# Holding back woven-in steps ahead of a long attention visit, loading two gate factors a unit earlier, and dealing the first score fills 4, 3, 3

## The chip, the cores and the metric

The kernel runs on one core of a Trainium2 chip. Its time is the device time of one execution in microseconds (us), median of several runs. The core has five engines that work side by side, each through its own instructions in order: TensorE (PE in the profile; PEld is its weight load), VectorE (DVE), ScalarE (ACT), GpSimd (POOL) and SyncE (SP, which here only issues DMAs). TensorE writes its results into PSUM, which this kernel uses as eight banks of 128 partitions x 512 floats; a bank can be written again once the engines that read it are done.

## The reference

All in float32, with x of 2048 x 640:

```
q, k, v = x wq, x wk, x wv           # 32 heads of 20, in 4 segments of 512 rows
per segment s and head:
    a_dot = softmax(q k^T / sqrt(20) + causal mask) v
    a_mem = (phi(q) M) / (phi(q) z + 1e-6)        # phi(t) = t+1 if t>0 else exp(t)
    o     = g a_mem + (1 - g) a_dot               # g = sigmoid(beta), per head
    M    += phi(k)^T v ;  z += sum phi(k)
a   = o wo
b   = (silu(x w1) * (x w3)) w2                    # inner width 1728
out = G a + (1 - G) b                             # G = sigmoid(x . gate_w), per row
```

## The kernel before, in words

The 2048 rows are four chunks of 512 (a chunk is a segment); the chunks go in two pairs, A = (0, 1) and B = (2, 3). A value that needs more precision than one pass gives is held as a high and a low part, and a product is three passes over them (`PASSES`), so a 640-wide projection of one 128-column block is 5 x 3 = 15 matmuls of 128 x 512.

Two streams of work share TensorE. The first is dense work: projections q, k, v; the feed-forward part (`ffn_up`, tiles g and u; `ffn_down`, tile f); the output projection (`oproj`, tile op); and small pieces woven into them. The second is attention, four heads (a *unit*) after another, 32 units. The order on TensorE is the order in which the Python code emits it; the order on the other engines is chosen by the framework's scheduler when the kernel is built.

**Attention visits.** `attention` (L792 on) counts slots, 40 to a unit. In slot 5 stands the *long visit* (`BIG`): three s fills, four t fills and the o product. In slot 17 stands the *short visit* (`SMALL`): s, t, s. An s fill (L634) puts scores of two heads into two banks, and VectorE scans them for row maxima (L641). A t fill (L667) puts transposed scores into two banks; ScalarE takes their exponential into P (L673) and GpSimd masks it (L677). The o product (L687) takes one bank. Unit 1 is an exception: its slot 5 has the first three fills only, and a further visit in slot 11 has the other four.

**Banks.** `bank_tile` gives the eight banks in turn: the one given longest ago comes next. A dense accumulation *holds* its bank until its last matmul, when `filled` puts it at the end of the row.

**Slots and credit.** The main loop at the end of the function gives, after every slot, a credit (declared cost of the segment's dense work divided by its slots) and draws dense steps while the credit is positive. A step is mostly three matmuls and declares 699 ns. Ahead of a visit of four or more pieces (place "between") it draws up to eight steps more, until no bank is held; ahead of a smaller one ("amid") up to four, until a bank has been held for two steps. What is drawn there is taken off the credit that follows.

**Weaving.** `braid(a, b, every, skip, rest)` yields the steps of a and puts one step of b behind every so many of them. Woven in like this are:

- `normalize` (L761 to L769; tiles rr, gt, on): for each of five 128-row blocks one matmul of row factors (rr), for chunks 1 to 3 also four transposes of memory's part (gt), each in a bank of its own; VectorE multiplies and adds (L762, L767), ScalarE casts (L768), VectorE subtracts (L769). In unit 10 for chunk 0, unit 19 for chunk 1, units 26 and 27 for chunk 2, and in the tail for chunk 3.
- `memory_read` (tile nd, L352): eight steps of six matmuls with three small VectorE operations each. In units 0 and 1 for chunk 1, 16 and 17 for chunk 2, 19 to 21 for chunk 3.
- `split_x` (L130 to L132, tile xh): x of chunks 2 and 3 is split into high and low parts, in unit 12 and at the start of 13.
- `load_memory` (L749): memory's part is loaded through GpSimd's queue.

**Gate factors.** `load_share(c)` (L740) loads the factors of chunk c, spread over 128 partitions (tile sh), on ScalarE's DMA queue. `share` (L543) multiplies the result by them. For chunk 0 it is called when its last `ffn_down` starts, for chunk 1 when the output projection starts after normalization, for chunks 2 and 3 in the tail.

## Time and profile before

| | |
|---|---|
| median of 3 runs | 1105.04 us (1104.69 to 1105.52) |
| profiled execution | 1107.25 us |
| its span on the core | 1105.4 us |
| TensorE clock granted in it | 1.00 |
| busy: PE / DVE / POOL / ACT | 1094.9 / 598.1 / 584.6 / 381.3 us |
| DMA | 153.20 MB, 139 GB/s mean |

The profile is one execution. A row of its timeline has the start in us from the start of the span, the duration, the engine, the line of the kernel, the operation, the tile written and those read, the shape and the number of merged instructions; in brackets stands how long the engine had been idle and what ended that. Matmuls are pipelined: each of 128 x 512 shows some 0.4 us, but the next starts after 0.23. So where time is lost on TensorE is read from start to start, not from its busy time.

### The profile page before, as it was taken

The page shows a single profiled execution, that of the slowest core. Times are in us where ns is not written, and L with a number is a line of the kernel's source. Part 1 is how long each engine was busy: PE and PEld are TensorE (multiplying, and loading weights), DVE is VectorE, ACT ScalarE, POOL GpSimd, SP SyncE. Part 2 cuts the span into 40 slices and gives each one's busy share as a digit, 9 for nine tenths or more (in the row PEclk, how much of TensorE's full clock was granted, in tenths as well). Part 3 has the DMA queues.
Part 4 walks back from the last instruction along what each step waited for, and adds up shares of the span by engine and source line. Part 5 has one row for each costly group of instructions (what it writes and reads, how often), then busy time and mean ns, then how long its engine had stood idle before and what let it go on. Part 6 is the DMA issues. An engine that isn't in the chain of part 4 may idle for free.

```text
span 1105.4 us, 17904 instructions
## 1 busy us (share of the span) xinstructions
PE 1094.9 (99%) x6290; PEld 853.0 (77%) x6290; DVE 598.1 (54%) x1711; ACT 381.3 (34%) x826; POOL 584.6 (53%) x729
## 2 busy tenths in 40 slices
PE   9999999999999999999999999999999999999998
PEld 6988877777777777787977777777777777777787
DVE  5032564356555554366153678875557665651575
ACT  6244233343233122145244543325333332223020
POOL 5055556366366363565066447556774665655263
PEclk9999999999999999999999999999999999999999
DMA  8256943334355134435367966365664343433122
GB/s 306 110 205 220 281 125 82 95 82 116 77 142 129 51 84 123 126 94 171 121 197 265 288 215 183 97 161 146 151 159 109 85 116 96 117 103 89 52 79 95
DMA packets 87545, 153.20 MB, mean 139 GB/s; under 512 B 11584, under 2 KB 25184, under 8 KB 87456
## 3 DMA queue, kind: packets, MB, share of 16 engines
q1 hardware_dynamic: 63040, 106.30, 30.1%
q0 software_dynamic: 20384, 38.68, 15.9%
q10 hardware_dynamic: 4032, 7.08, 1.8%
q8 instruction: 50, 0.82, 0.3%
q14 instruction: 39, 0.32, 0.1%
HBM read 96.56 MB, written 54.54 MB: 137 GB/s over the span
## 4 chain that ended last, share of the span: by engine, by line
PE 93%; DVE 4%; ACT 1%; DMA 1%; issue 1%; ACTq 0%; SPq 0%; DVEq 0%
PE g L257 16%; PE f L580 16%; PE u L257 16%; PE k L257 6%; PE v L385 6%; PE op L837 6%; PE o L687 6%; PE q L257 5%; PE s L634 5%; PE t L667 4%; PE nd L352 1%; PE pm L449 1%; PE q L327 1%; DVE junk L641 1%; DMA sh<-ed 1%
## 5 line engine op out<-in xcount | busy, mean ns | idle before, releaser
L641 DVE CUSTOM_DVE_ANT_0 junk<-s,mask 128x256 bf16<-128x256 f32 (+3 forms) x512 | 250.3, 489 | 105.9 <-PE s L634 73.6
L673 ACT ACTIVATE P<-t 128x512 f32<-128x512 f32 (+1 forms) x384 | 172.5, 536 | 190.2 <-PE t L667 153.0
L257 PE MATMUL g<-X,W 128*128 128x512 f32 x840 | 208.5, 398 | 0.0
L179 POOL TENSOR_TENSOR W<-wr,W 128x640 fp32r<-128x640 f32 (+1 forms) x126 | 198.5, 1581 | 2.5
L174 POOL CAST W<-wr 128x640 fp32r<-128x640 f32 (+1 forms) x126 | 92.5, 739 | 202.0 <-PE f L580 47.7
L580 PE MATMUL f<-ht,W 128*128 128x512 f32 (+1 forms) x825 | 197.0, 395 | 0.7 <-DVE acc L550 0.7
L257 PE MATMUL u<-X,W 128*128 128x512 f32 x780 | 196.7, 399 | 0.0
L677 POOL TENSOR_SCALAR_AFFINE_SELECT P<-P 128x256 f32<-128x256 f32 x192 | 94.6, 502 | 183.2 <-ACT P L673 182.9
L257 PEld LDWEIGHTS g<-X,W 128*128 128x128 f32 x840 | 155.9, 188 | 36.6 <-issue 0.4
L580 PEld LDWEIGHTS f<-ht,W 128*128 128x128 f32 x825 | 152.9, 188 | 37.6 <-DVE acc L550 1.5
L257 PEld LDWEIGHTS u<-X,W 128*128 128x128 f32 x780 | 144.0, 188 | 34.4 <-ACT P L673 0.3
L107 POOL TENSOR_TENSOR ht<-ft,ht 128x512 fp32r<-128x512 f32 x52 | 67.2, 1291 | 90.1 <-ACT ht L106 90.0
L611 POOL DMA_DIRECT2D qk<-qkd x128 | 83.6, 655 | 0.5 <-issue 0.2
L634 PE MATMUL s<-qk 60*128 60x256 f32 (+3 forms) x512 | 77.8, 345 | 1.1 <-DVE fu L520 1.0
L257 PE MATMUL k<-X,W 128*128 128x512 f32 x300 | 77.0, 403 | 0.0
L687 PE MATMUL o<-P,vg 128*32 128x512 f32 (+3 forms) x1024 | 75.5, 435 | 1.4 <-DVE on L767 1.4
L519 ACT ACTIVATE ft<-g 128x512 f32<-128x512 f32 x52 | 31.2, 599 | 124.9 <-PE g L257 113.8
L385 PE MATMUL v<-W,X 128*128 128x320 f32 (+1 forms) x480 | 71.9, 311 | 0.3 <-ACT P L673 0.3
L520 DVE SCALAR_TENSOR_TENSOR fu<-ft,g 128x512 f32<-128x512 f32 x52 | 35.7, 686 | 67.3 <-ACT ft L519 58.3
L385 PEld LDWEIGHTS v<-W,X 128*128 128x128 f32 x480 | 71.0, 189 | 1.0 <-ACT P L673 0.5
L106 ACT CAST ht<-ft 128x512 fp32r<-128x512 f32 x52 | 32.2, 619 | 110.9 <-DVE ft L528 110.8
L588 DVE TENSOR_TENSOR acc<-f,acc 128x512 f32<-128x512 f32 x65 | 44.7, 689 | 44.8 <-PE f L580 44.6
(123 smaller groups left out, 1204.8 us busy)
## 6 DMA issues: line engine op xcount, KB each, us to landing
qk<-qkd POOLq DMA_DIRECT2D x128, 240.0 KB, 4.0
wr<-in_w_dram SPq DMA_DIRECT2D x80, 320.0 KB
qkd<-qs SPq DMA_DIRECT2D x20, 512.0 KB
qkd<-ks SPq DMA_DIRECT2D x20, 512.0 KB
od<-oq SPq DMA_DIRECT2D x32, 256.0 KB
wr<-in_wo_dram SPq DMA_DIRECT2D x20, 320.0 KB
vg<-vd SPq DMA_DIRECT2D x16, 336.0 KB
xr<-in_xT_dram SPq DMA_DIRECT2D x20, 256.0 KB
```

The source lines that it names most:

```text
L107: (lo or nc.gpsimd.tensor_sub)(dst[:, 1], src, dst[:, 0].bitcast(F32))
L174: hi = nc.gpsimd.tensor_copy(w[:, 0, :n], raw[:, :n])
L179: last["low"] = nc.gpsimd.tensor_sub(w[:, 1, :n], raw[:, :n], w[:, 0, :n].bitcast(F32))
L257: nc.tensor.matmul(ps, w[:, a, kb * P:(kb + 1) * P], x[:, b, kb, :], start=n == 0, stop=n == 14)
L385: nc.tensor.matmul(ps[:, :n1 - n0], x[:, a, kb, lb * P:(lb + 1) * P], wvt[kb][:, b, n0:n1], start=n == 0, stop=n == 14)
L580: nc.tensor.matmul(ps[:, :n1 - n0], w, h, start=n == 0, stop=n == len(ms) - 1)
L611: here(nc.gpsimd.dma_start(t[64 * i:64 * i + RH], qkd[c][RH * (h + i):RH * (h + i + 1)]))
L634: nc.tensor.matmul(ps[i][:, o:o + w], q[:, qb * P:(qb + 1) * P], key[:, :w], start=n == 0, stop=n == len(todo) - 1, skip_group_check=True)
L641: nc.vector.tensor_tensor_reduce(out=junk[:, :w], in0=ps[i][:, o:o + w], in1=mask[:, L - w:], scale=1.0, scalar=-3.0e38, op0=ALU.add, op1= ...
L673: last["exp"] = nc.scalar.activation(pairs[2 * m + k]["P"][:, i, o:o + n], ps[i][:, b:b + n], AF.Exp, scale=SCALE)
L677: nc.gpsimd.affine_select(d, d, pattern=[[0, 2], [0, n], [1, P]], base=0, channel_multiplier=-1, compare_op=ALU.is_ge, fill=0.0)
L687: nc.tensor.matmul(ps[32 * i:32 * i + 32, kb * P:], heads[2 * p + i]["v"][:, kb], pairs[p + i // 2]["P"][:, i % 2, o:o + n], start=kb == 0 ...
```

## The change

Three edits. First, `braid` counts the woven-in steps that are due, and emits one only while `near()` is false; `near()` is true while the slot counter stands at 2 to 5 of a unit, that is in the draws after slots 1 to 4 and in those made ahead of the long visit in slot 5. A step that fell due there comes behind a later step of a, one at a time. Second, the factors of chunk 0 are loaded ahead of the last up projections of pair A, those of chunk 1 ahead of chunk 1's normalization; for chunks 2 and 3 the call stays where it is, in a function that takes the chunks. Third, in unit 1 the fill ("t", 1, 3) moves from the visit in slot 11 to that in slot 5, so that unit 1's three visits have four, three and three fills; by their sizes the first now counts as "between" and the second as "amid".

```diff
@@ ffn_down
         for c in cs:
-            if c in last and c < 2:
-                load_share(c)
             if first:
@@
-    def both_shares():
-        for c in B:
+    def load_shares(cs):
+        for c in cs:
             load_share(c)
             yield 1
@@ attention
-                todo = VISITS.get(n, ()) if m != 1 else {BIG: VISITS[BIG][:3], BIG + 6: VISITS[BIG][4:]}.get(n, VISITS.get(n, ()))
+                todo = VISITS.get(n, ()) if m != 1 else {BIG: VISITS[BIG][:3] + VISITS[BIG][4:5], BIG + 6: VISITS[BIG][5:]}.get(n, VISITS.get(n, ()))
@@ oproj
         def first():
+            if c == 1:
+                load_share(c)
             yield from normalize(c)
...
         def rest():
             ws.extend(w_get(i, plan[0]) for i in plan)
-            if c == 1:
-                load_share(c)
@@
+    def near():
+        return BIG - 3 <= (slots - LEAD) % 40 <= BIG
+
     def braid(a, b, every, skip=0, rest=True):
 
         def gen():
-            n = 0
+            n = due = 0
             for y in a[1]:
                 yield y
                 n += not isinstance(y, float)
-                if n > skip and (n - skip) % every == 0:
+                due += n > skip and (n - skip) % every == 0
+                if due and not near():
+                    due -= 1
                     z = next(b[1], None)
                     if z is not None:
                         yield z
@@
     A, B = (0, 1), (2, 3)
+    slots = 0
@@ segment of pair A's end
-    seg += [(0, load_raw(2)), (0, load_raw(3))] + u0 + [braid(chain(u1), (0, x2), 4, 0, False)]
+    seg += [(0, load_raw(2)), (0, load_raw(3)), (0, load_shares(A[:1]))] + u0 + [braid(chain(u1), (0, x2), 4, 0, False)]
@@ tail
-    tail = [braid(chain([d, (0, both_shares())] + u), o1, 4, 10)] + [braid(o2, (0, shared(2)), 3), job_down(B, 4, B)]
+    tail = [braid(chain([d, (0, load_shares(B))] + u), o1, 4, 10)] + [braid(o2, (0, shared(2)), 3), job_down(B, 4, B)]
@@ main loop
-    slots, credit = 0, 0.0
+    credit = 0.0
```

## The prediction

> **What bounds the kernel now.** I read the page's engine shares and chain first, then the list of TensorE's waits, then the timeline of TensorE around each named place, and last VectorE's timeline there.

> ```profile
> span 1105.4 us, 17904 instructions
> PE 1094.9 (99%) x6290; PEld 853.0 (77%) x6290; DVE 598.1 (54%) x1711; ACT 381.3 (34%) x826; POOL 584.6 (53%) x729
> PE 93%; DVE 4%; ACT 1%; DMA 1%; issue 1%; ACTq 0%; SPq 0%; DVEq 0%
> ```

> TensorE is busy for the whole span and carries 93% of the chain of waits. The change keeps all 6290 matmuls, so only the time between their starts can move. The undisturbed pace is the yardstick: rows of unit 18 (long visit, short visit) and two rows of projection work.

> ```profile
> 679.59 0.50 PE L634 MATMUL s<-qk 60*128 60x512 f32 x2
> 684.09 3.73 PE L257 MATMUL g<-X,W 128*128 128x512 f32 x15
> 689.14 0.50 PE L634 MATMUL s<-qk 60*128 60x256 f32 x4
> 690.10 1.20 PE L257 MATMUL u<-X,W 128*128 128x512 f32 x4
> ...
> 473.39 7.13 PE L257 MATMUL g<-X,W 128*128 128x512 f32 x30
> 480.36 1.54 PE L257 MATMUL u<-X,W 128*128 128x512 f32 x6
> ```

> From start to start, a long visit takes 684.09 - 679.59 = 4.50 us, a short one 690.10 - 689.14 = 0.96 us, and thirty wide matmuls 6.97 us, 0.232 us each. What lies above this is waiting, and little of it is left in the whole trace; the change aims at three places.

> **Part 1, the first t fills (unit 1).** The second visit of unit 1 has four fills now:

> ```profile
> 152.60 0.50 PE L667 MATMUL t<-qk 62*128 62x512 f32 x2
> 153.41 0.33 PE L634 MATMUL s<-qk 60*128 60x384 f32 x1
> ...
> 153.99 0.68 DVE L520 SCALAR_TENSOR_TENSOR fu<-ft,g 128x512 f32<-128x512 f32 x1
> 154.72 0.50 PE L634 MATMUL s<-qk 60*128 60x384 f32 x3 [0.98 <-DVE fu L520]
> ```

> Four fills take eight banks. The eighth is the bank that the g projection has just closed, and VectorE's fu (0.68) still reads it. The two matmuls of this pair normally start together; here they are 154.72 - 153.41 = 1.31 us apart. Some 1.25 us is lost. With three fills in this visit only six banks are taken and that wait goes: -1.25. In its place the first visit takes all eight banks and comes right after u: its last t fill needs u's bank, and the memory step that the pause puts behind it needs the bank of the first s fill, which VectorE must scan first. No row shows this order. Lower bound 0 (VectorE's work fits), upper bound 1.31 (the same wait, moved). I take 0.5: one VectorE operation like that fu, 0.68, is ahead of that scan, and I guess 0.2 of it covered. Part 1: -0.75, between -1.25 and +0.06.

> **Part 2, the gate factors.** Chunk 0's load (sh) is issued when the down projection starts, and VectorE, first in first out, stops at its first use:

> ```profile
> 495.39 9.38 PE L580 MATMUL f<-ht,W 128*128 128x512 f32 x40
> 496.37 0.32 ACTq L740 DMA_DIRECT2D sh<-ed  x1
> 503.12 1.29 DVE L543 TENSOR_TENSOR acc<-acc,sh 128x512 f32<-128x512 f32 x2 [3.35 <-DMA sh<-ed]
> 505.07 1.44 PE L580 MATMUL f<-ht,W 128*128 128x512 f32 x5 [0.30 <-DVE acc L550]
> 512.34 0.51 PE L634 MATMUL s<-qk 60*128 60x512 f32 x2
> 517.85 1.45 PE L385 MATMUL v<-W,X 128*128 128x320 f32 x8 [0.30 <-ACT P L673]
> ...
> 495.39:517.85 22.46, 18.09 (x34) 1.00 0.48 161
> ```

> The load takes 503.12 - 496.37 = 6.75 us; VectorE idles 3.35 of them. TensorE pays later, when it needs banks: from 495.39 to 512.34 stand 65 wide matmuls, 15.1 us at 0.232, in 16.95 us: 1.85 lost. The long visit of unit 13 takes 5.51 instead of 4.50: 1.01 lost. Together 2.86. Issued ahead of the two g projections, at about 473.39, the load has 23 us more, over three times its 6.75, even beside the raw inputs loaded just before; ScalarE's issue is 0.32 us as before. The last row (a stretch; VectorE busy for 18.09 of 22.46 us) shows that VectorE can keep up once the hole is closed: 4.37 us are idle, 3.35 of them the hole. What stays: it runs with little slack, two splits of x now fall behind the visit, and the v projection then starts on a bank that waits for a scan instead of an exponential. I leave 0.86 for that, between 0 and 2.0 (the 1.01 of the visit and half of the 1.85). Part 2: -2.0, between -2.86 and -0.86. Chunk 1's factor causes no wait now, and the last two loads stay where they are: 0.

> **Part 3, the pause.** Normalization in unit 19:

> ```profile
> 699.88 0.39 PE L761 MATMUL rr<-rR,sel 96*128 96x512 bf16 x1
> 701.33 0.50 PE L634 MATMUL s<-qk 60*128 60x512 f32 x2
> 702.85 0.68 DVE L767 TENSOR_TENSOR on<-on,gt 128x512 f32<-128x512 f32 x1
> 703.28 1.28 POOL L107 TENSOR_TENSOR ht<-ft,ht 128x512 fp32r<-128x512 f32 x1 [5.75 <-ACT ht L106]
> 703.45 1.66 DVE L769 TENSOR_TENSOR oall<-on,gm 128x512 fp32r<-128x512 f32 x1
> 703.68 2.36 PE L687 MATMUL o<-P,vg 128*32 128x512 f32 x32 [1.38 <-DVE on L767]
> 707.40 1.66 PE L257 MATMUL g<-X,W 128*128 128x512 f32 x6
> 707.71 0.43 POOL L677 TENSOR_SCALAR_AFFINE_SELECT P<-P 128x256 f32<-128x256 f32 x1 [1.95 <-ACT P L673]
> 708.90 0.39 PE L761 MATMUL rr<-rR,sel 96*128 96x512 bf16 x1
> 709.49 2.34 PE L257 MATMUL g<-X,W 128*128 128x512 f32 x9
> 711.67 0.39 PE L761 MATMUL rr<-rR,sel 96*128 96x512 bf16 x1
> ```

> The step at 699.88 holds the bank that the visit's o product needs. The visit takes 707.40 - 701.33 = 6.07 us, 1.57 above 4.50. The pause covers four slots of 0.374 us credit (103.5 us of declared work over 277 slots), about two steps of 0.70, so this step is held back: -1.57. Counting slots and declared costs on, its turn goes to the next projection step. That opens g of the other chunk, and a long visit doesn't start while an accumulation is open, so all five steps of g run ahead of the visit. They are missing behind it: between long and short visit there are then only norm, three u matmuls, norm: 0.59 (708.90 to 709.49) + 0.73 (a third of 709.49 to 711.67) + 0.59 = 1.91 us, where nine steps stand now. Each norm takes two banks, so the short visit reaches, beside the banks of the long visit's last scans, those of both norms. VectorE has to finish first:

> ```profile
> 687.10 0.08 DVE L641 DVE_READ_ACCUMULATOR2_ANT m<- 128x1 f32 x1
> ...
> L762 DVE TENSOR_TENSOR on<-oall,rr x20: 671/680/682, 384.5 to 1052.6; 128x512 f32<-128x512 f32 x20
> ...
> L769 DVE TENSOR_TENSOR oall<-on,gm x15: 679/693/1660, 698.4 to 1056.1; 128x512 fp32r<-128x512 f32 x15
> ```

> In unit 18 the scans end at 687.18, 3.09 us after the visit. To them come two L762 and one L767, 2.04 us, and their ends come 4.5 (if 0.6 fits into gaps between scans) to 5.1 us after the visit. The short visit wants the last of these banks 0.6 us after its start, at 2.5. New wait: 2.0 to 2.6, I take 2.3. Bounds: 0.5 (rows of units 17 and 20 below) and 6.65 (the second rival). Part 3 in unit 19: -1.57 + 2.3 = +0.75, between -1.1 and +5.1.

> The memory steps are held back too, in units 16 to 17 and 19 to 21:

> ```profile
> 661.63 0.99 PE L352 MATMUL nd<-Ms,pq 128*128 128x84 f32 x6
> 663.96 0.51 PE L634 MATMUL s<-qk 60*128 60x256 f32 x4
> 665.42 0.77 PE L352 MATMUL nd<-Ms,pq 128*128 128x147 f32 x4
> 732.39 0.50 PE L634 MATMUL s<-qk 60*128 60x256 f32 x4
> 733.88 0.74 PE L837 MATMUL op<-gm,W 128*128 128x512 f32 x2
> ```

> These two short visits take 1.46 and 1.49, 0.5 above 0.96. In unit 17 two more memory steps will stand before the short visit; it comes 3.6 instead of 2.33 us behind the long one (663.96 - 661.63) and VectorE has time: -0.4. In unit 20 one is added, with as much VectorE work as it gives time: +0.1. Together -0.3, between -1.0 and +0.8. The memory's loads on the POOL queue keep their order behind the steps they follow; SP's stores shift by steps, and nobody waits for them. Counted the same way, no step of units 10, 26, 27 or 31 falls into the pause, and the slot counter ends outside it, so that the tail keeps its order: 0.

> **Sum.** -0.75 - 2.0 + 0.75 - 0.3 = -2.3 us. The profiled execution took 1107.25 us (span 1105.4 and 1.85 around it) and would take 1104.95; it lay 2.2 above the median of the runs, so against 1105.04 the forecast is 1102.7. About 0.2%, 2.2 us, is what a measurement of this kernel tells from no change.

> **Rivals.** First, all waits go and nothing new comes: -1.25 - 2.86 - 1.57 - 1.0 = -6.7, so 1098.4. For it speaks that VectorE is busy for only 54%; against it that unit 19's short visit comes 1.91 us behind a long one and needs five banks more.

> Second, the other side: VectorE's pile-up in unit 19 is deeper. If its queue sets whole norms ahead, the short visit waits for two L769 as well, each up to 1.66: 3.09 + 4 x 0.68 + 2 x 1.66 = 9.15, less 2.5 = 6.65, 4.35 more than I took. If the output projection then also waits for the fifth norm, about a wide accumulation's quarter, 0.9 us, it is 1107.9. It decides from a new wait of 4.6 us on. L769 speaks for it: its longest, 1.66, is the one at 703.45 in this very stretch, but the median is 0.693. [...]

> Third, the load's hole isn't the cause: VectorE stays behind in unit 13 because chunk 0 asks of it two operations per five matmuls (1.38 us against 1.16) and the splits beside them. Then part 2 brings only 0.86, and the time is 1103.9, which no measurement tells from before. Against it: the 4.37 idle us.

> **How the numbers follow.** Forecast 0.45, its own range 1101.4 to 1104.0 (part 3 from 1.0 to 3.6 of new wait); all waits go 0.18; VectorE's pile-up 0.25; the hole isn't the cause 0.12. The forecast lies at the 0.2% line: of its 0.45, 0.29 are faster and 0.16 within. Faster 0.18 + 0.29 = 0.47; within 0.16 + 0.12 = 0.28; slower 0.25. The range reaches halfway into the first two rivals: 1099.8 to 1106.4.

> **What would show it.** Right: no wait for sh on VectorE and the long visit of unit 13 below 5.0 us; the pair at 153 together; long visit of unit 19 at 4.5 with fifteen g matmuls just before it, and a short visit there of about 3.2 instead of 1.0. Wrong: that short visit under 1.5 (first rival), or over 5.5 (second).

## The result, and the profile after

The changed kernel takes 1107.26 us (1106.4 to 1108.49, 11 runs), the kernel before, on the same chip, 1105.0 (11 runs): ratio 1.0016, 95% interval 1.0009 to 1.0024. By the medians it is slower by 2.3 us where 2.3 us faster was forecast. (A ratio here is worked out over all runs; it is not the quotient of the two medians.)

In the code after the change the lines named in the prediction stand two lower from `ffn_down` on: an s fill is L632, a t fill L665, the o product L685, VectorE's scan L639, the normalization L759 to L767, the load of the gate factors L738. From the page of the kernel after, the engines' busy time and the chain by engine:

```profile
PE 1094.6 (99%) x6290; PEld 855.0 (77%) x6290; DVE 599.0 (54%) x1711; ACT 381.3 (34%) x826; POOL 583.5 (53%) x729
PE 96%; DVE 1%; ACT 1%; DMA 0%; issue 0%; SPq 0%; DVEq 0%
```

TensorE's share of the chain has grown from 93 to 96%, and that of waits for VectorE and DMA has shrunk from 5 to 1%. Nothing in these lines looks worse. What is worse shows only in the places themselves, on TensorE's timeline of the kernel after (units 1, 13 and 19):

```profile
146.73 0.50 PE L632 MATMUL s<-qk 60*128 60x512 f32 x2
147.07 1.01 PE L665 MATMUL t<-qk 62*128 62x512 f32 x8
...
151.91 0.40 PE L632 MATMUL s<-qk 60*128 60x384 f32 x4
...
509.70 0.50 PE L632 MATMUL s<-qk 60*128 60x512 f32 x2
515.53 1.74 PE L385 MATMUL v<-W,X 128*128 128x320 f32 x10 [1.15 <-DVE m L639]
...
701.61 0.51 PE L632 MATMUL s<-qk 60*128 60x512 f32 x2
...
706.13 0.39 PE L759 MATMUL rr<-rR,sel 96*128 96x512 bf16 x1
...
708.50 0.38 PE L632 MATMUL s<-qk 60*128 60x256 f32 x1
709.05 0.50 PE L632 MATMUL s<-qk 60*128 60x256 f32 x3 [0.17 <-DVE m L639]
711.54 0.57 PE L665 MATMUL t<-qk 62*128 62x384 f32 x4 [1.99 <-DVE m L639]
711.90 0.74 PE L632 MATMUL s<-qk 60*128 60x384 f32 x4
712.58 1.65 PE L257 MATMUL u<-X,W 128*128 128x512 f32 x3
714.03 0.65 PE L759 MATMUL rr<-rR,sel 96*128 96x512 bf16 x1
```

Read from start to start. Unit 1: the pair that stood 1.31 us apart is closed (the four matmuls from 151.91 on stand in one row, with no wait). Unit 13: the long visit takes 5.83 us (before 5.51) but starts 28.64 us after the short visit of unit 12 instead of 30.51; the v projection behind it now waits for a scan. Unit 19: the long visit takes 4.52 (before 6.07), the short one 712.58 - 708.50 = 4.08 (before 1.02), with 2.70 us of waiting ahead of its t fill (711.54 - 708.50 = 3.04 where 0.34 is normal); it starts 2.37 us behind the long one (708.50 - 706.13), where 1.91 was counted. And what follows is odd: from 711.54 on every matmul takes twice its time, three u matmuls 1.45 us (712.58 to 714.03) instead of 0.73. Three stretches of the kernel after, in time order (length in us, then busy time of each engine with its instruction count, the granted clock, the DMA share and GB/s), show why:

```profile
708.42:711.83 3.41, 1.25 (x10) 0.77 (x9) 3.27 (x11) 1.14 (x2) 1.05 (x2) 1.00 0.99 261
711.84:715.25 3.41, 3.41 (x17) 2.38 (x13) 3.05 (x14) 1.18 (x3) 1.94 (x4) 0.50 0.06 11
715.26:718.66 3.40, 3.40 (x17) 2.81 (x16) 2.92 (x9) 0.90 (x3) 1.34 (x2) 1.00 0.65 145
```

The granted TensorE clock is 0.50 for 3.41 us, right after 3.41 us in which TensorE was busy for 1.25. Half of 3.41, 1.7 us, is TensorE time lost to the clock. Now the stretch from the end of unit 18's short visit to the end of unit 20's, first before, then after:

```profile
690.10:733.88 43.78, 42.30 (x281) 31.17 (x277) 36.01 (x109) 17.51 (x40) 23.70 (x31) 1.00 0.42 111
```

```profile
687.56:733.70 46.14, 43.96 (x281) 32.23 (x277) 34.38 (x108) 17.31 (x39) 23.28 (x31) 0.96 0.38 104
```

The same 281 matmuls take 2.36 us longer; 1.66 of it is busy time, which is what 3.41 us at half clock cost (1.7). The other stretches between these two profiled executions, start to start: up to the long visit of unit 2 (from the first attention matmul) -0.82, unit 13 -1.55, units 16 and 17 -0.42, unit 18 +0.17, the rest within 0.1. The sum is -0.3, and the spans differ by -0.2. The profiled execution of before lay 2.2 above its median, that of after (1107.26) on it; where those 2.2 us come from is taken up under "The load, once more".

### The profile page after: what moved, and what is told of

It reads as the page before. It is cut to its first block, busy times and chain, and to the rows that moved or that the text cites. A ratio compares the mean times of both kernels' runs of the same rounds, so it can differ in the third digit from the quotient of the medians.

```text
span 1105.2 us, 17895 instructions
## 1 busy us (share of the span) xinstructions
PE 1094.6 (99%) x6290; PEld 855.0 (77%) x6290; DVE 599.0 (54%) x1711; ACT 381.3 (34%) x826; POOL 583.5 (53%) x729
## 4 chain that ended last, share of the span: by engine, by line
PE 96%; DVE 1%; ACT 1%; DMA 0%; issue 0%; SPq 0%; DVEq 0%
PE g L257 18%; PE f L578 17%; PE u L257 17%; PE op L835 6%; PE k L257 6%; PE v L385 6%; PE o L685 6%; PE q L257 5%; PE s L632 5%; PE t L665 4%; PE nd L352 2%; PE pm L449 1%; PE q L327 1%; PE gt L764 1%; PE pkt L434 1%; DVE junk L639 0%
## 5 line engine op out<-in xcount | busy, mean ns | idle before, releaser
L639 DVE CUSTOM_DVE_ANT_0 junk<-s,mask 128x256 bf16<-128x256 f32 (+3 forms) x512 | 250.4, 489 | 104.3 <-PE s L632 71.5
L257 PE MATMUL g<-X,W 128*128 128x512 f32 x840 | 208.8, 398 | 0.0
L257 PE MATMUL u<-X,W 128*128 128x512 f32 x780 | 196.7, 400 | 0.0
L257 PEld LDWEIGHTS g<-X,W 128*128 128x128 f32 x840 | 156.0, 188 | 36.3
L257 PEld LDWEIGHTS u<-X,W 128*128 128x128 f32 x780 | 144.8, 189 | 34.5 <-issue 0.4
L107 POOL TENSOR_TENSOR ht<-ft,ht 128x512 fp32r<-128x512 f32 x52 | 67.0, 1289 | 89.7 <-ACT ht L106 89.6
L632 PE MATMUL s<-qk 60*128 60x256 f32 (+3 forms) x512 | 77.3, 347 | 0.2 <-DVE m L639 0.2
L257 PE MATMUL k<-X,W 128*128 128x512 f32 x300 | 77.1, 404 | 0.0
L685 PE MATMUL o<-P,vg 128*32 128x512 f32 (+3 forms) x1024 | 75.5, 436 | 0.2
L520 DVE SCALAR_TENSOR_TENSOR fu<-ft,g 128x512 f32<-128x512 f32 x52 | 35.6, 685 | 69.2 <-ACT ft L519 58.9
L385 PE MATMUL v<-W,X 128*128 128x320 f32 (+1 forms) x480 | 71.9, 311 | 1.2 <-DVE m L639 1.2
L385 PEld LDWEIGHTS v<-W,X 128*128 128x128 f32 x480 | 71.0, 189 | 1.9 <-DVE m L639 1.4
L106 ACT CAST ht<-ft 128x512 fp32r<-128x512 f32 x52 | 32.2, 619 | 111.9 <-DVE ft L528 111.9
```

The source lines that it names most:

```text
L107: (lo or nc.gpsimd.tensor_sub)(dst[:, 1], src, dst[:, 0].bitcast(F32))
L257: nc.tensor.matmul(ps, w[:, a, kb * P:(kb + 1) * P], x[:, b, kb, :], start=n == 0, stop=n == 14)
L385: nc.tensor.matmul(ps[:, :n1 - n0], x[:, a, kb, lb * P:(lb + 1) * P], wvt[kb][:, b, n0:n1], start=n == 0, stop=n == 14)
L632: nc.tensor.matmul(ps[i][:, o:o + w], q[:, qb * P:(qb + 1) * P], key[:, :w], start=n == 0, stop=n == len(todo) - 1, skip_group_check=True)
L639: nc.vector.tensor_tensor_reduce(out=junk[:, :w], in0=ps[i][:, o:o + w], in1=mask[:, L - w:], scale=1.0, scalar=-3.0e38, op0=ALU.add, op1= ...
L685: nc.tensor.matmul(ps[32 * i:32 * i + 32, kb * P:], heads[2 * p + i]["v"][:, kb], pairs[p + i // 2]["P"][:, i % 2, o:o + n], start=kb == 0 ...
```

## The experiments

Times are medians beside runs of the kernel before on the same chip: its median is 1105.16 beside the kernel before again, the loads, the loads with the fills, and the pause; 1105.42 beside the fills alone, the memory's pause, the normalization's pause and the zeros; 1105.32 beside the two kernels whose pause lasts until the short visit is over; 1105.47 beside the rest. Ratios have their 95% interval.

**The kernel before again**, with no edit.

> The kernel before, once more. Two theories. Rows theory: the two traces are typical, so VectorE again idles 3.3 us for sh, the long visit of unit 13 takes 5.5 and that of unit 19 6.1 us, span 1105.4. Odd-run theory: the profiled execution of before lay 2.2 us above the median because a wait in it was longer than usual; then this trace has a span near 1103 and one of these waits is 1 to 2 us shorter. Time by both: 1105.0, no difference.

1105.86 us, ratio 1.0003 (0.9994 to 1.0012). The profiled execution took 1108.97, and its wait for sh is there again (3.1 us); neither theory holds whole, since the long wait is there but the span is 1107.1, not 1105.4 or 1103.

**The parts alone.** Only the loads moved (the move of chunk 1's load, as in the change, isn't printed again):

```diff
-            if c in last and c < 2:
-                load_share(c)
...
-    seg += [(0, load_raw(2)), (0, load_raw(3))] + u0 + [braid(chain(u1), (0, x2), 4, 0, False)]
+    seg += [(0, load_raw(2)), (0, load_raw(3)), (0, load_shares(A[:1]))] + u0 + [braid(chain(u1), (0, x2), 4, 0, False)]
```

> Only the gate factors' loads are moved. Rows theory: the two traces stand 1.5 us closer behind the long visit of unit 13 than ahead of unit 12, so 1103.5. Odd-run theory: the hole is usually shorter and little is gained, 1104.5 to 1105.0.

Only the fills (the part of the line that differs):

```diff
-{BIG: VISITS[BIG][:3], BIG + 6: VISITS[BIG][4:]}
+{BIG: VISITS[BIG][:3] + VISITS[BIG][4:5], BIG + 6: VISITS[BIG][5:]}
```

> Only the t fills are dealt 4, 3, 3. From the difference of the two kernels with moved loads: 1.0 us faster than before, 1104.2. Odd-run theory, now for the load of the gate factors: it waits longer in a profiled execution than in a plain one, so the profiled execution of this kernel lies about 2 us above its own median, as before's do, and shows a wait for sh of 3 us; with the loads moved no such distance was seen. Rival: the median itself is 1.5 to 2 us above that with the loads moved, 1105.5.

Both of these edits:

> The loads moved and the t fills dealt 4, 3, 3, no pause. Rows theory: 0.8 us more than the loads alone bring, 1102.7. Odd-run theory: 1104 to 1105.

Only the pause:

```diff
+    def near():
+        return BIG - 3 <= (slots - LEAD) % 40 <= BIG
...
-                if n > skip and (n - skip) % every == 0:
+                due += n > skip and (n - skip) % every == 0
+                if due and not near():
+                    due -= 1
```

> Only the pause. Rows theory: unit 19 loses 2.1 us (its long visit 1.57 shorter, its short visit 3.1 longer, then 3.4 us at half the clock), 1107. If instead the half clock is what the change costs and it is bound to the pause alone, the mean clock is 0.998 here and 1.000 in the two runs without the pause. If the loss sat elsewhere, the clock would be 1.000 here and the time near 1105.

| only | us | ratio to before |
|---|---|---|
| loads | 1104.9 | 0.9996 (0.9988 to 1.0005) |
| fills | 1104.32 | 0.9995 (0.9987 to 1.0004) |
| loads and fills | 1103.94 | 0.9987 (0.9978 to 0.9996) |
| pause | 1110.15 | 1.0038 (1.0026 to 1.0050) |

By the ratios the pause alone costs 4.2 us, twice the 2.1 that were expected of it: in its profiled execution the clock is halved for two windows behind the short visit of unit 19 instead of one, and the long visit of unit 18 takes 5.74 us instead of 4.50. The fills' gain is below what the times tell, and the loads bring nothing that can be measured in them; both together bring 1.4 us. That is nearer to the second theory, in which the long wait for sh is not the usual one. That profiling itself makes the load longer, as expected for the fills alone, didn't come out: their profiled execution (1103.85) lies below their median and waits 1.1 us. The profiles tell more of the fills. From the end of the first attention visit to the long visit of unit 2 stand 45.4 us in the five profiles with neither the fills nor the pause, 44.4 in the three with the fills where memory's steps don't pause, and 44.3 in the seven with both. So the fills bring 1.0 us and the pause 0.1 more. The times hide it, since the first visit itself takes 0.89 to 2.05 us in the sixteen profiles, and 0.90 to 2.05 in the three of the kernel before alone. In the second and third profile of the kernel before, it waits for the DMA that brings qk:

```profile
127.91 0.70 PE L634 MATMUL s<-qk 60*128 60x512 f32 x5 [0.68 <-DMA qk<-qkd]
...
126.79 0.70 PE L634 MATMUL s<-qk 60*128 60x512 f32 x5 [0.22 <-DMA qk<-qkd]
```

**Which steps must not pause.** The changed kernel, with a switch at each use of `braid`; first only the memory steps (and the splits of x) pause, then only the normalization. The first is shown, at one of the uses; in the second the default is `hold=False`, and the uses for normalization get `hold=True`:

```diff
-    def braid(a, b, every, skip=0, rest=True):
+    def braid(a, b, every, skip=0, rest=True, hold=True):
...
-                if due and not near():
+                if due and not (hold and near()):
...
-    seg = [braid(up[2], o1, 3), braid(o2, job_read(3), 3, 1), job_down(B, 0), braid(chain(jobs_up(B, 1)), (0, load_memory(2)), 5)]
+    seg = [braid(up[2], o1, 3, hold=False), braid(o2, job_read(3), 3, 1), job_down(B, 0), braid(chain(jobs_up(B, 1)), (0, load_memory(2)), 5)]
```

> The change, but normalization doesn't pause; memory's steps and the splits of x do. Theory (the loss is normalization's held-back steps in unit 19): clock 1.000, unit 19 as without a pause (long visit 5.4, short 1.0), the short visits of units 17 and 20 some 0.4 us shorter, time 1103.0 to 1103.9. Rival (any pause costs, since it pushes dense work ahead of the long visit): 1105 or more.

> The change, but only normalization pauses. Theory: the whole loss is here: short visit of unit 19 about 4.1 us, mean clock 0.997 to 0.998, 1107.5 to 1108. Rival: 1104 to 1105.

Memory alone pausing: 1103.65, ratio 0.9986 (0.9977 to 0.9994). Normalization alone: 1108.28, ratio 1.0028 (1.0016 to 1.0039). Against 1103.94 with neither, the memory's pause is worth nothing that can be measured and that of the normalization costs 4.3 us; against the changed kernel, taking it away brings 3.6. So the loss is the normalization's pause, and in the profiles it lies in unit 19. Two windows at half clock follow its short visit with only the normalization pausing (the second opens although TensorE was busy for 2.74 of 3.40 us in the first half-clock window):

```profile
709.91:713.31 3.40, 1.82 (x12) 1.17 (x12) 3.11 (x12) 1.71 (x3) 0.12 (x1) 1.00 0.63 142
713.32:716.72 3.40, 2.74 (x10) 2.27 (x10) 3.19 (x13) 0.56 (x1) 2.11 (x4) 0.50 0.36 84
716.73:720.14 3.41, 3.41 (x10) 2.64 (x9) 2.38 (x9) 0.79 (x4) 0.96 (x2) 0.50 0.32 62
```

**The clock's share.** The changed kernel, with twelve products that add zero to an open accumulation, put where the short visit of unit 19 waits:

```diff
+                        if (m, n, kind, f) == (19, SMALL, "s", [3]):
+                            for _ in range(12):
+                                nc.tensor.matmul(open_u[3, 2][:, :384], mask[:, :P], mask[:, :384],
+                                                 start=False, stop=False, skip_group_check=True)
```

> The change, and in unit 19's short visit, behind its first s fill, twelve matmuls of zeros of 128 x 384 that add nothing to the open accumulation of u: 1.9 us of work just where TensorE stands idle for 2.0. Theory (two costs: the wait, and half the clock for 3.4 us because TensorE was idle in most of a window before): the short visit stays at 4.1 us, the clock stays at 1.000, time 1.7 us below the change's, 1105.5. Rival (the half clock is free, because VectorE is what everything waits for there): 1107.2 as with the change, clock 1.000.

1106.34, ratio 1.0008 (1.0000 to 1.0017): 0.9 less than the changed kernel, about half of what was expected. The clock stays at 1.00 in every execution (0.996 to 0.998 in every one of the changed kernel). TensorE's timeline with the zeros (here t is L666, gt L765) shows why it isn't 1.7:

```profile
708.80 2.12 PE L810 MATMUL u<-mask 128*128 128x384 bf16 x12
710.85 0.50 PE L666 MATMUL t<-qk 62*128 62x384 f32 x4
...
712.38 0.39 PE L760 MATMUL rr<-rR,sel 96*128 96x512 bf16 x1
713.42 0.66 PE L765 MATMUL gt<-ident,gm 128*128 128x128 f32 x4 [0.65 <-DVE m L640]
```

The t fill starts 5.42 us behind the long visit, as in the changed kernel (711.54 - 706.13 = 5.41), so the zeros themselves, 2.05 us from 708.80 to 710.85, cost nothing. But the next step of normalization, 1.5 us later, now waits 0.65 us for VectorE. At half clock that wait lay hidden: in the changed kernel this gt starts at 714.47 without a wait, 2.93 us behind the t fill (711.54); here it starts 2.57 us behind it (713.42 - 710.85), the wait included.

**What the short visit waits for.** VectorE's timeline in the kernel after, from 0.9 us behind the long visit on:

```profile
707.03 0.68 DVE L760 TENSOR_TENSOR on<-oall,rr 128x512 f32<-128x512 f32 x1
...
708.11 0.68 DVE L765 TENSOR_TENSOR on<-on,gt 128x512 f32<-128x512 f32 x1
...
708.92 0.68 DVE L760 TENSOR_TENSOR on<-oall,rr 128x512 f32<-128x512 f32 x1
...
709.99 0.68 DVE L767 TENSOR_TENSOR oall<-on,gm 128x512 fp32r<-128x512 f32 x1
710.60 0.68 DVE L765 TENSOR_TENSOR on<-on,gt 128x512 f32<-128x512 f32 x1
...
711.40 0.08 DVE L639 DVE_READ_ACCUMULATOR2_ANT m<- 128x1 f32 x1
```

VectorE has hardly a gap (busy for 3.27 of the 3.41 us from 708.42 on). Five operations of the two steps between the visits stand among the scans, and the last scan frees its bank at 711.48, when t starts. Two theories: the short visit comes too soon behind the long one, or these two steps may not stand between. Four kernels bear on it. All five steps ahead of the long visit (changed against the kernel whose normalization doesn't pause):

```diff
-braid(up[2], o1, 3, hold=False)
+braid(up[2], o1, 1, hold=False)
```

> The changed kernel, but the normalization neither pauses nor is spread out: in unit 19 one of its steps follows every projection step, so that all five stand ahead of the long visit and none between the two visits. If the price of the pause is that two steps of normalization stand 1.9 us ahead of a short visit that needs their banks, that price is gone here, and so is the 0.86 us that the long visit loses where normalization steps stand just before it (5.36 against 4.50): some 0.9 us under the kernel whose normalization doesn't pause (1103.65), so 1102.8, with a long visit of 4.5 to 4.7 and a short one of 0.96 in unit 19. Rival: five steps of about 2 us of VectorE work each, packed into some 6 us of TensorE work, pile up on VectorE, and the long visit or the projection before it waits for them: a long visit of 5.5 or more, 1103.7 to 1105.

A step every two projection steps, with the pause:

```diff
-braid(up[2], o1, 3)
+braid(up[2], o1, 2)
```

> The changed kernel, but the normalization of unit 19 comes every two projection steps instead of every three, and still pauses: three steps stand ahead of the long visit and two behind it, as many behind as in the changed kernel, but with twelve projection matmuls between the visits instead of three. If the short visit waits because it comes 1.9 us behind the long one, while VectorE needs 5.4 us from there for the bank that it wants last, then here it comes about 4.0 us behind and waits under 1 us (a short visit of 1.0 to 1.9 instead of 4.08), the clock isn't halved, and the time is 1103 to 1104. Rival: it is the two held-back steps themselves that VectorE can't take beside its scans, wherever the short visit stands: the wait moves to the g matmuls or stays at 2 us, and the time is 1106 or more.

The pause of unit 19 drawn out until the short visit is over, with a step every three, then every two projection steps:

```diff
-    def near():
-        return BIG - 3 <= (slots - LEAD) % 40 <= BIG
+    def near(end):
+        return BIG - 3 <= (slots - LEAD) % 40 <= end
...
-    def braid(a, b, every, skip=0, rest=True):
+    def braid(a, b, every, skip=0, rest=True, end=BIG):
...
-braid(up[2], o1, 3)
+braid(up[2], o1, 3, end=SMALL)
```

> The changed kernel, with the pause of unit 19's normalization drawn out until the short visit is over, still every three projection steps: the short visit comes even sooner behind the long one (six projection matmuls, 1.46 us, instead of 1.9), but with no normalization step between. If those steps are what the short visit waits for in the changed kernel (4.08 us long), it now waits for the scans of the long visit alone, which end 3.1 us behind it: a short visit of 2.0 to 2.5, no window at half clock, and what is left is how far the output projection waits for the last of the three late steps (0.5 to 2 us): 1104.5 to 1106. Rival: the short distance is the cause, whatever stands between: the short visit is as long as in the changed kernel or longer (4 us), the clock is halved, 1107 or more.

```diff
-braid(up[2], o1, 3)
+braid(up[2], o1, 2, end=SMALL)
```

> The changed kernel, with the normalization of unit 19 every two projection steps and its pause drawn out until the short visit is over: three steps ahead of the long visit, none between the visits (21 projection matmuls stand there), two behind the short one. If the normalization steps between the visits are the whole price of the pause, both visits of unit 19 are undisturbed here (4.5 and 0.96), against 4.51 and 1.68 with two steps between them 4.1 us apart (1103.79): 0.7 us less, 1103.1; if the output projection waits some tenths for the two late steps, 1103.5. Rival: the two steps, now 0.7 to 2 us ahead of the output projection that needs the whole result, hold it up by the 2 us that a step takes on VectorE: 1104.5 to 1105.5, and the pause only has three places to put the same loss in.

Unit 19 in their profiled executions (steps of normalization ahead of, between and behind the visits; time between the two visits; length of each; the lowest clock granted):

| kernel | steps | between | long | short | clock | median us | ratio to before |
|---|---|---|---|---|---|---|---|
| before | 3, 2, 0 | 6.42 | 6.07 | 1.02 | 1.00 | 1105.0 | 1 |
| normalization doesn't pause | 3, 2, 0 | 6.42 | 5.36 | 1.02 | 1.00 | 1103.65 | 0.9986 (0.9977 to 0.9994) |
| changed | 2, 2, 1 | 2.37 | 4.52 | 4.08 | 0.50 | 1107.26 | 1.0016 (1.0009 to 1.0024) |
| every two | 3, 2, 0 | 4.47 | 4.51 | 1.68 | 1.00 | 1103.79 | 0.9985 (0.9976 to 0.9994) |
| every three, none between | 2, 0, 3 | 1.59 | 4.51 | 1.54 | 0.50 | 1109.94 | 1.0039 (1.0025 to 1.0053) |
| every two, none between | 3, 0, 2 | 5.06 | 4.51 | 0.96 | 1.00 | 1103.24 | 0.9979 (0.9970 to 0.9988) |
| all five ahead | 5, 0, 0 | 2.98 | 8.40 | 0.96 | 0.50 | 1106.99 | 1.0012 (1.0004 to 1.0021) |

With two steps between as before, but 2.1 us more of projection there (and one step more ahead of the long visit, none behind the short one), 4.08 turns into 1.68. Taking the steps away and leaving the short distance shortens the short visit even more than I expected (1.54, expected 2.0 to 2.5), but then the steps themselves wait, on TensorE's timeline of that kernel:

```profile
709.57 0.38 PE L759 MATMUL rr<-rR,sel 96*128 96x512 bf16 x1 [0.52 <-DVE m L639]
710.62 0.66 PE L764 MATMUL gt<-ident,gm 128*128 128x128 f32 x4 [0.67 <-DVE m L639]
...
714.99 0.38 PE L759 MATMUL rr<-rR,sel 96*128 96x512 bf16 x1 [1.65 <-DVE m L639]
717.00 0.66 PE L764 MATMUL gt<-ident,gm 128*128 128x128 f32 x4 [1.64 <-DVE m L639]
```

That is 4.48 us of idle time against 2.2 in the changed kernel (46.14 - 43.96), and the time is over 1107, which is the rival's. So neither theory holds alone: the short visit's own wait goes with the steps (1.54 us at an even shorter distance), but the loss stays and moves to the steps. The reading that fits all seven rows is this: two visits and the steps beside them ask VectorE for one lump of work, and whoever comes next for a bank waits until it is done, unless projection matmuls, which ask VectorE for little (one operation of 0.7 us per fifteen), stand between. Steps and distance change together in these kernels, so the share of each is not measured apart. The same at the other end: with all five steps ahead of the long visit, that visit waits, and it is my expectation of 1102.8 that failed there; the 1106.99 lie above the rival's 1103.7 to 1105 too:

```profile
701.32 0.50 PE L665 MATMUL t<-qk 62*128 62x384 f32 x3 [0.54 <-DVE on L760]
703.22 3.82 PE L685 MATMUL o<-P,vg 128*32 128x512 f32 x32 [1.40 <-DVE on L765]
```

The best kernel gives the lump room at both ends (three steps spread out ahead, 21 projection matmuls between the visits, two steps behind). TensorE in it:

```profile
703.14 3.76 PE L257 MATMUL g<-X,W 128*128 128x512 f32 x15
706.74 1.54 PE L257 MATMUL u<-X,W 128*128 128x512 f32 x6
708.20 0.50 PE L632 MATMUL s<-qk 60*128 60x256 f32 x4
```

At 1103.24 us it is faster than both kernels. That it beats the two at 1103.65 and 1103.79 is not shown.

**The load, once more.** The moved load gained 1.55 us in unit 13 against the profiled execution of before, and nothing in the medians. The kernel before was profiled again, and another kernel was to issue the load later:

> The kernel before, once more, for a profile. The two profiled executions of it so far took 1107.25 and 1108.97 us, 2.2 and 3.1 above their medians, and the load of chunk 0's gate factors flew 6.7 and 6.4 us in them; in the profile of the kernel with the fills alone, which issues that load at the same place, it flew 4.5 us, VectorE waited 1.1 us for it and TensorE not at all. If the length of that flight differs from one execution to the next, and a wait of 3.3 us is the slower kind, a profiled execution near 1105 shows a flight of about 4.5 us and no wait of TensorE in the down projection before unit 13, and one near 1107 shows 6.5. Rival: the flight is always 6.5 us in this kernel, and the fills alone shorten it by their shift; then it is 6.4 or more here too, whatever the time.

```diff
-            if c in last and c < 2:
+            if c in last and c == 1:
                 load_share(c)
...
+                    if c in last and c == fb == 0:
+                        load_share(c)
                     filled()
```

> The kernel before, but the load of chunk 0's gate factors is issued five projection matmuls (1.16 us) later. If VectorE's wait for it is just covered in most executions (1.1 us of waiting, nothing lost on TensorE), 1.2 us more uncovers some of it: 0.3 to 1.3 us slower than before, 1105.5 to 1106.5. If the whole wait of VectorE already cost TensorE time, as the prediction had it, it is 1.0 to 1.2 slower. If TensorE doesn't depend on it at all, the time is that of before, 1105.2.

The second took 1105.44, ratio 1.0000 (0.9991 to 1.0010), but its edit did nothing: the load was issued 14.5 us behind the short visit of unit 12, as in the kernel before (496.37 - 481.83), so it says nothing of a late load, only that there are two more profiles with the load at its old place. The rows of its tile around unit 13, with the wait for it, in the kernel before profiled again, and then in the kernel with the fills alone:

```profile
L543 DVE TENSOR_TENSOR acc<-acc,sh x5: 686/689/2028, 501.9 to 509.1; 128x512 f32<-128x512 f32 x5
L740 ACTq DMA_DIRECT2D sh<-ed x1: 321/321/321, 497.3 to 497.3; - x1
  DMA sh<-ed: 1.2, 1
```

```profile
L543 DVE TENSOR_TENSOR acc<-acc,sh x5: 685/686/711, 499.7 to 506.9; 128x512 f32<-128x512 f32 x5
L740 ACTq DMA_DIRECT2D sh<-ed x1: 321/321/321, 495.2 to 495.2; - x1
  DMA sh<-ed: 1.1, 1
```

| load at its old place, profiled execution | issue to first use, us | VectorE waits | unit 12's short visit to v |
|---|---|---|---|
| before | 6.7 | 3.3 | 36.02 |
| before, second profile | 6.4 | 3.1 | 35.72 |
| before, third profile | 4.6 | 1.2 | 35.18 |
| pause alone | 4.7 | 1.3 | 34.47 |
| fills alone | 4.5 | 1.1 | 33.78 |
| edit without effect | 4.5 | 1.1 | 33.81 |

With the load moved this stretch takes 34.3 to 34.5 us in all ten profiles. So the wait of 3.3 us, on which part 2 rested, is one of two lengths that these executions show; where it is 1.1 to 1.3 us, TensorE loses nothing in the f matmuls ahead of the visit. In one and the same order (the kernel before and the edit without effect) the long load costs 36.02 - 33.81 = 2.2 us. With only the load moved the stretch is 34.36: 1.7 us less than with the long load, but 0.55 more than with the short one. The third profile doesn't bear out that the length of the load alone decides the time of an execution: it took 1107.31 us with a load of 4.6. Its stretch has an L543 of 2.03 us, and 0.7 us more than in the first profile were lost between the first attention matmul and unit 2 (172.83 - 125.84 against 171.93 - 125.60): that is its first visit, 1.57 us long instead of 0.90, with the wait for qk shown above. What makes these loads longer in some executions is open.

## Why the prediction was wrong

Between the forecast of 1102.7 and the 1107.26 lie 4.6 us: 2.1 are unit 19 (part 3) and 2.2 the base that the forecast was set against (part 2); the rest nearly cancels.

- **Part 1, right.** Forecast -0.75, with 0.5 of new wait in unit 1's first visit. That visit takes 1.46 us for ten matmuls, the last 0.5 of it waiting, as said. The stretch up to unit 2 is 0.82 shorter; the very first attention visit, which the change leaves alone, took 0.34 longer in this execution, so unit 1 itself gained 1.16, of which the fills are 1.0. By the ratio of the times the fills alone are -0.5 us (interval -1.4 to +0.4).
- **Part 2, wrong in what it was set against.** Against the profiled execution the step held nearly: -1.55 for a forecast -2.0; the waits for sh and of the f matmuls are gone. The long visit of unit 13 was to fall below 5.0 and takes 5.83. What is new there is in the row of the factors in the kernel after: one of the five products takes 2.06 us, beside a GpSimd addition. That this keeps the visit long is not shown: with the pause alone the visit takes 5.83 too, and there no such product is longer than 0.69.

```profile
L543 DVE TENSOR_TENSOR acc<-acc,sh x5: 678/687/2064, 497.7 to 506.7; 128x512 f32<-128x512 f32 x5
...
497.74 3.05 DVE L543 TENSOR_TENSOR acc<-acc,sh 128x512 f32<-128x512 f32 x2
...
498.33 1.91 POOL L179 TENSOR_TENSOR W<-wr,W 128x642 fp32r<-128x642 f32 x1
```

  What makes that product long is not shown. L769, now L767, which the second rival took at up to 1.66 apiece, took 0.68 at 709.99. The larger error is the step from 1104.95 to 1102.7: the 2.2 us by which the profiled execution lay above the median were taken off the forecast, although the wait that part 2 removes was part of what made that execution slow (36.02 against 33.81 us in the table above). By the ratio of the times the load is worth -0.4 us (interval -1.3 to +0.6).
- **Part 3, the step that failed.** The order came out as counted: fifteen g matmuls ahead of the long visit, two steps and three u matmuls behind it. The long visit's -1.57 is -1.55. The new wait was forecast at 2.3 (2.0 to 2.6) and is 2.70: by the time the last scan ends VectorE has done five operations of the steps, not three (two L760, two L765 and one L767, against two L762 and one L767 of the old numbering); that scan ends 5.35 us behind the long visit, where 4.5 to 5.1 was forecast. The short visit takes 4.08 where 3.2 was the sign. The term that was missing altogether is the clock: 1.7 us of TensorE time, of which taking the half clock away brings 0.9 us in the result. Sum for unit 19: -1.55 + 2.70 + 1.7 = +2.85, for a forecast of +0.75.
- **Memory's steps.** Unit 17 gave 0.42 as said and unit 20 0.52, which was said to lose 0.1; unit 18 lost 0.17. By the medians it is nothing. Unit 18 is a cost that the forecast didn't have: in the eight profiles whose memory steps pause its long visit takes 4.66 to 5.74 us, in the eight others 4.50. The o product waits there; for what, the profiles don't name.
- **The sum.** Against its own base the forecast was -2.3 and the profiled executions differ by 0.0: unit 19 was 2.1 short, part 2 0.45 and unit 18 0.17, unit 20 gave 0.6 more than said, and 0.2 came outside the span. The other 2.2 are the base. The outer range of 1099.8 to 1106.4 doesn't follow from the figures given for it: halfway from 1101.4 and 1104.0 to the two rivals is 1099.9 and 1105.95; the result lies above both.
- **The rivals.** The second, VectorE's pile-up, gave 1107.9, close to the 1107.26, but that is luck, not what happened: it took a wait of 6.65 and asked for 4.6 at least. With a wait of 2.70 the time came out as high because the clock was lost behind it and because the forecast's base, which this rival shared, was 2.2 too low. "All waits go" could nearly be had in units 1 and 19, with the pause drawn out and a step every two, and gives 1103.24, not 1098.4: 2.86 of its 6.7 us were the load's, of which the medians show none. The third, 1103.9 because the load's hole isn't the cause, was right that part 2 would bring little, for a reason of its own: with the wait gone the visit of unit 13 is still 5.83 long, and in most profiles of the old place the wait is the short one.

## What to carry to other kernels

A wait taken from a profiled execution that lies above the median may be the very thing that puts it there: profile the kernel twice before a gain is counted on, and then count it against one base only. Work that is held back does not vanish from the queue of the engine behind it: where VectorE is the one to catch up, look at how much TensorE work that asks little of it stands between one user of the banks and the next; the fast kernels of the table have some 4.5 us or more there, and no lump on the other side. And a wait on TensorE should be priced with what the clock may take behind it: here 2.70 us of waiting in unit 19 were followed by 3.41 us at a clock of 0.50, 1.7 us of TensorE time.

## What the runs showed of the hardware

The forecast had no term for the clock. In the profile of the changed kernel the record of the granted clock has 1.00 for 706.56 us, 0.50 for 3.41 (711.84 to 715.25), and 1.00 for 389.12, until behind the end of the work; at 3.4133 us to a step these are 207 steps, one, and 114, so in this execution the changes keep to one grid. In the first profile of the kernel before it has 1.00 for 1099.09 us, 322 such steps. With the pause alone and with only the normalization pausing the half clock lasts two steps (713.07 to 719.88 and 713.32 to 720.14). Rows of windows one step long, stepped back by 3.41 us from the half clock, from two more kernels (the one with all five steps ahead; the one with none between and every three):

```profile
699.43:702.83 3.40, 1.85 (x11) 0.86 (x9) 3.40 (x8) 2.02 (x4) 0.66 (x2) 1.00 0.00 0
702.85:706.25 3.40, 3.03 (x20) 0.99 (x24) 1.58 (x4) 1.16 (x3) 1.40 (x2) 0.50 0.02 5
```

```profile
711.19:714.59 3.40, 2.15 (x12) 1.38 (x12) 3.40 (x10) 0.62 (x1) 1.01 (x2) 1.00 1.03 213
714.60:718.01 3.41, 1.38 (x8) 0.92 (x8) 2.85 (x12) 1.00 (x3) 0.00 (x0) 1.00 0.03 5
718.02:721.42 3.40, 3.40 (x10) 2.64 (x9) 2.40 (x6) 1.14 (x2) 1.29 (x2) 0.50 0.02 5
```

and one behind which the clock stays full (the fills alone):

```profile
698.08:701.49 3.41, 2.01 (x16) 0.99 (x20) 3.41 (x7) 3.34 (x7) 1.46 (x2) 1.00 0.01 2
```
